# A wider planned margin for what TensorE takes from other engines, and for reused buffers, in the later stages

## The chip, the cores and the metric

The kernel runs on one core of a Trainium2 chip. The metric is the device time of one execution in microseconds. Three runs of the kernel before gave 1037.63, 1038.01 and 1040.27 us; the median is 1038.01 us. One more execution was taken with the hardware profiler; all rows of the profile below come from it. In the rows PE is TensorE's matmuls, PEld its weight loads, DVE is VectorE, ACT is ScalarE, POOL is GpSimd and SP is the engine that issues the DMAs. L1176 is line 1176 of the kernel.

## The reference

Causal attention with a decay bias, and behind it a two-layer network with an ELU between the layers:

```python
batch, n_heads, seq, head_dim = (8, 8, 576, 64)
n_tokens, d_model, d_ff = (4608, 512, 2048)

scores = scale * np.matmul(q, k.transpose(0, 1, 3, 2))
cum = np.cumsum(np.maximum(s, 0.0), axis=-1)
bias = -(cum[:, :, :, None] - cum[:, :, None, :])
scores = np.where(causal, -1000000000.0, scores + np.minimum(bias, 0.0))
scores = scores - np.max(scores, axis=-1, keepdims=True)
attn = np.exp(scores)
attn = attn / (np.sum(attn, axis=-1, keepdims=True) + 1e-09)
x = np.matmul(attn, v)                      # (8, 8, 576, 64)
x = x.transpose(0, 2, 1, 3).reshape(4608, 512)
h = x @ w_in                                # 512 -> 2048
g = np.where(h > 0.0, h, np.exp(np.minimum(h, 0.0)) - 1.0)
out = g @ w_out                             # 2048 -> 512
```

All tensors are 32-bit floats. There are 64 heads (8 batches of 8), and the network sees 4608 tokens of 512 features.

## The kernel before, in words

**Attention.** The work is cut into units. For most batches a unit is one head with up to four blocks of 128 queries. For a block, `softmax_block` (from L1165 on) makes the scores in a PSUM bank by two matmuls (L1176, tiles `kh` and `qs`, then `k` and `q`); VectorE adds the mask, takes the running minimum and empties the bank (L1179, tiles `p` and `mn`); ScalarE takes the exponential (L1189). Then the probabilities are scaled and split into a high and a low half of 16 bits: the high half at L1247, L1249 or L1251 (GpSimd, VectorE or ScalarE), the low half mostly at L1255 on VectorE. SP issues DMA transposes of the halves into `T`, and `heads` (L1396) multiplies them with the values of two heads into the bank `av`. `produce` (L833, L835, L840) turns `av` into the network's input `x`, again in halves. Keys and queries are rounded at L405 and L407, and what is left of them is made at L426 on GpSimd or L425 on VectorE; L1039 makes the low half of the values.

**The network.** Tokens are handled in 18 chunks of 256. A chunk has 8 steps (two blocks of 128 hidden features each). A step has a hidden part, 24 matmuls of 256 columns at L1636 into a bank `h`, issued as 8 operations of three; then ScalarE's exponential (L1654), a subtraction with a limit (L1663 on VectorE or L1659 on ScalarE), VectorE's L1667, the high half `gg` (L1671 or L1673) and its low half (L1676); then the projection, 12 matmuls of 512 columns at L1697 into two banks `o`, as two operations of six. The first chunks (L1573, L1603) use whole 32-bit operands instead. At a chunk's end the banks `o` are copied out (L1734, L1736) and stored.

**PSUM.** Scores, transposes and the small end products share two banks (tag `a`, `N_A` = 2), in the first stages a third one. The hidden parts have two banks and later that third one; the projections have two (`N_O` = 2), `av` has one.

**The order.** All of this is entered as operations in a planner, `Plan`, and `plan.issue()` writes the program. The planner simulates the engines by a cost for each operation (the functions `pe16`, `dve_2` and so on). Again and again it takes, of all operations whose inputs are planned, the one with the earliest start, and among those with the same start the one with the smallest priority number. Its start is the latest of three: when its engine is free (`free`), when its inputs are known there (`ready`, the planned end of each input plus a handover of `HOPS` that depends on the two engines, 150 ns if not listed), and when a slot of each new buffer is free (`slot_free`, the end of the last user plus `HOP` = 150 ns). On TensorE attention comes first by priority (small numbers, in the order of the units), the network's matmuls have 10000 plus the chunk's number, so they fill in what attention leaves. On the other engines the network's own work (-1000 plus the chunk) comes ahead of attention's. Where an operation can be done by several engines, the planner takes the one where it ends first.

What is written is an order for each engine, which the engine keeps; the real waits are semaphores and depend on the data alone. So a number in the planner changes what stands ahead of what, and never adds a wait by itself. A planned time has no meaning on the chip beyond that order.

Two constants already depend on the planned time of TensorE: `THIRD_T` (165 us) moves the third bank from scores to hidden parts, and `FIRST_T` (180 us) changes a weight in the choice of engines.

Of the kernel before, what the change touches and what calls it, by code (L numbers as in the profile page):

```python
# [54 lines left out]
N_FREE = 0  # L55
N_EARLY, N_AUX, N_URGENT = 2, 4, 1

FILL_T, GAP = 60e3, 350.0

N_FILL = 300  # L60
# [29 lines left out]
class Plan:  # L90
# [14 lines left out]
        ("Pool", "Pool"): 50.0,  # L105
    }
    HOP = 150.0

    BIAS = {"DVE": 1.3, "DVE-SB": 1.3}
    FIRST_BIAS = {"DVE": 1.3, "DVE-SB": 1.3}  # L110
# [59 lines left out]
        return o  # L170

    def ready(self, o, engine):
        return max(
            (t + (0.0 if e is None else self.HOPS.get((e, engine), self.HOP))
             for e, t in o.ready.items()),
            default=0.0,
        )

    def issue(self):
        engines = sorted({self.ENGINE.get(w[0], w[0]) for o in self.ops for w in o.ways})  # L180
        port = 0.0
        free = dict.fromkeys(engines, 0.0)
        taken = dict.fromkeys(self.tags, 0)
        slots, skipped = {}, {}
# [2 lines left out]
        def slot_free(key, bufs):  # L187

            held = slots.get(key, ())
            if len(held) < bufs:  # L190
                return 0.0
            was = held[-bufs]
            return None if was.users else was.until + self.HOP

        pending = [o for o in self.ops if not o.left]
        block = self.nc.cur_bb.bb
# [2 lines left out]
        while pending:  # L199
# [12 lines left out]
            for o in pending:  # L212
                t = 0.0
                for b, k in o.new:
                    at = None
                    if b.home_bufs and taken[b.home] == k:
                        b.key, b.bufs = b.home, b.home_bufs
                        at = slot_free(b.key, b.bufs)
                    if b.others and (b.always or not busy):
                        for key, bufs, *rule in b.others:  # L220
                            if rule and not rule[0](taken[key]):
                                continue
                            other = slot_free(key, bufs)
                            if other is not None and (at is None or other < at):
                                at, b.key, b.bufs = other, key, bufs
                    if at is None:
                        break
                    t = max(t, at)
                else:
                    _, n, start = min(  # L230
                        (at + w[1] * bias.get(w[0], 1.0), i, at)
                        for i, w, at in (
                            (i, w, max(t, free[self.ENGINE.get(w[0], w[0])],
                                       self.ready(o, self.ENGINE.get(w[0], w[0])),
                                       port - self.PORT_LEAD[w[0]] if w[0] in self.PORT_LEAD else 0.0))
                            for i, w in enumerate(o.ways)
                        )
                    )
                    rank = (start + GAP if o.filler else start, o.prio)
                    if best is None or rank < best[0]:  # L240
                        best = (rank, o, n)
# [4 lines left out]
            engine, cost, trace = o.ways[n][:3]  # L246
            lag = 0.0
            end = start + cost
            if engine in self.PORT_LEAD:
                port = end  # L250
            engine = self.ENGINE.get(engine, engine)
# [1590 lines left out]
```

## Time and profile before

| | |
|---|---|
| median of 3 runs | 1038.01 us (1037.63 to 1040.27) |
| profiled execution | 1035.61 us, span 1033.7 us |
| busy TensorE / VectorE / ScalarE / GpSimd | 1014.4 / 834.6 / 627.0 / 386.1 us |
| granted clock of TensorE | 1.00 |
| instructions | 21490 |
| largest groups on TensorE | L1697 378.7 us (1608 matmuls), L1636 376.0 us (3072), L1176 with `kh` and `qs` 109.1 us (272) |
| DMA | 137.73 MB, 133 GB/s on average |

A row of a group reads: line, engine, operation, tile written <- tiles read, shape, count, then busy time and mean length in ns, then the engine's idle time just before such instructions and what ended it. In a row of the order of time the first two numbers are start and length in us, and what stands in brackets at the end is the idle time before it with the instruction that ended it. TensorE's matmuls overlap in its pipeline: a matmul of 512 columns has a length of 380 ns, but 36 of them take 7.78 us, 216 ns each.

### The profile page before, as it was taken

The numbers are of one execution on the slowest core, as the hardware profiler recorded it, in microseconds if no ns is written. First come the engines' busy times: TensorE is split into PE (matmuls) and PEld (weight loads), VectorE is DVE, ScalarE is ACT, GpSimd is POOL, SyncE is SP. The second block draws the span as 40 slices with busy tenths as digits, with TensorE's granted clock in tenths as the row PEclk, the third lists the DMA queues.
The fourth block names the chain that finished last, engine by engine and source line by source line (L and its number), as shares of the span: only waits on it lengthen the run. The fifth ranks groups of instructions, "written<-read, shape, count | busy, mean of one in ns | idle before, by whom it ended". The sixth has DMA issues, their size and how long they took to land.

```text
span 1033.7 us, 21490 instructions
## 1 busy us (share of the span) xinstructions
PE 1014.4 (98%) x7260; PEld 695.7 (67%) x7260; DVE 834.6 (81%) x2047; ACT 627.0 (61%) x1502; POOL 386.1 (37%) x605
## 2 busy tenths in 40 slices
PE   8999999999999999999999999999999999999998
PEld 6666766667676666676666666666676766676665
DVE  6889899999989999898899998888888888433333
ACT  4877756676666666766676666756666656333232
POOL 6332345464554445547556444423232322000000
PEclk9999999999999999999999999999999999999999
DMA  7767243779668677766787657747464544100000
GB/s 222 233 198 234 62 142 96 175 155 217 130 146 172 131 151 152 186 149 142 162 201 146 148 132 172 151 109 181 112 141 101 129 110 122 34 22 22 1 21 21
DMA packets 277693, 137.73 MB, mean 133 GB/s; under 512 B 211640, under 2 KB 254928, under 8 KB 277584
## 3 DMA queue, kind: packets, MB, share of 16 engines
q1 hardware_dynamic: 277584, 136.37, 54.8%
q8 instruction: 57, 0.93, 0.4%
q14 instruction: 52, 0.43, 0.1%
HBM read 68.63 MB, written 9.88 MB: 76 GB/s over the span
## 4 chain that ended last, share of the span: by engine, by line
PE 84%; DVE 9%; issue 3%; DMA 2%; ACT 1%; POOL 0%; SPq 0%; DVEq 0%; ACTq 0%; POOLq 0%
PE h L1636 30%; PE o L1697 30%; PE sc L1176 10%; PE av L1396 5%; PE o L1603 3%; PE h L1573 3%; DVE p L1255 2%; DVE v L1039 1%; DMA stk<-in_kT_dram 1%; PE trl L975 1%; PE avl L991 1%; DVE p L1179 1%; PE scratch L1760 1%; DVE g L1663 1%; DMA vs<-in_vb_dram 1%
## 5 line engine op out<-in xcount | busy, mean ns | idle before, releaser
L1697 PE MATMUL o<-wp,gg 128*128 128x512 f16 x1608 | 378.7, 380 | 1.0 <-DVE gg L1676 0.8
L1636 PE MATMUL h<-x,wp 128*128 128x256 f16 x3072 | 376.0, 273 | 0.0
L1636 PEld LDWEIGHTS <-wp 128*128 128x128 f16 x3216 | 301.8, 98 | 65.4 <-issue 8.4
L1697 PEld LDWEIGHTS <-gg 128*128 128x128 f16 x1608 | 151.3, 98 | 158.0 <-issue 3.9
L1255 DVE SCALAR_TENSOR_TENSOR p<-p,sm,p 128x512 f16<-128x512 f32 (+3 forms) x234 | 181.1, 789 | 5.3 <-POOL p L1247 2.4
L1189 ACT ACTIVATE p<-p,mn 128x192 f32<-128x192 f32 (+1 forms) x232 | 143.4, 619 | 43.8 <-DVE mn L1179 41.8
L1654 ACT ACTIVATE g<-h,cs 128x512 f32<-128x512 f32 x134 | 91.7, 684 | 111.5 <-PE h L1636 109.2
L1671 ACT ACTIVATE gg<-h,wc 128x512 f16<-128x512 f32 x122 | 83.6, 685 | 96.7 <-DVE h L1667 96.0
L1179 DVE CUSTOM_DVE_ANT_0 p<-sc,maskw 128x192 f32<-128x192 f32 (+1 forms) x232 | 109.2, 477 | 17.4 <-PE sc L1176 14.1
L1676 DVE SCALAR_TENSOR_TENSOR gg<-h,wc,gg 128x512 f16<-128x512 f32 x134 | 99.8, 745 | 25.8 <-ACT gg L1671 25.1
L1176 PE MATMUL sc<-kh,qs 128*128 128x192 f32 (+2 forms) x272 | 109.1, 405 | 7.0 <-DVE mn L1179 5.6
L1247 POOL TENSOR_SCALAR p<-p,sm 128x512 f16<-128x512 f32 (+3 forms) x105 | 61.1, 586 | 145.4 <-DVE sm L1198 104.0
L1667 DVE SCALAR_TENSOR_TENSOR h<-g,cs,h 128x512 f32<-128x512 f32 x134 | 100.6, 751 | 16.2 <-ACT g L1659 12.1
L1663 DVE TENSOR_SCALAR g<-g 128x512 f32<-128x512 f32 x77 | 37.2, 483 | 74.4 <-ACT g L1654 74.1
L1251 ACT ACTIVATE p<-p,sm 128x512 f16<-128x512 f32 (+3 forms) x114 | 67.6, 603 | 32.4 <-DVE sm L1198 30.9
L1176 PE MATMUL sc<-k,q 128*128 128x192 f32 (+2 forms) x272 | 83.2, 309 | 0.0
L1176 PEld LDWEIGHTS sc<-kh,qs 128*128 128x128 f32 x272 | 51.4, 189 | 28.4 <-DVE mn L1179 7.3
L426 POOL TENSOR_TENSOR qs<-stq,qs 64x512 fp32r<-64x512 f32 (+1 forms) x53 | 63.5, 1198 | 6.7 <-ACT qs L407 1.2
L426 POOL TENSOR_TENSOR k<-stk,kh 64x576 fp32r<-64x576 f32 x36 | 54.8, 1523 | 15.3 <-ACT kh L407 11.8
L1396 PE MATMUL av<-T,v 128*64 128x256 f16 (+5 forms) x896 | 60.3, 286 | 0.0
L405 POOL TENSOR_SCALAR qs<-stq 128x512 fp32r<-128x512 f32 (+1 forms) x42 | 27.9, 664 | 72.9 <-DMA stq<-in_qT_dram 51.6
L1176 PEld LDWEIGHTS sc<-k,q 128*128 128x128 f32 x272 | 51.8, 190 | 1.9
(216 smaller groups left out, 1326.1 us busy)
## 6 DMA issues: line engine op xcount, KB each, us to landing
stk<-in_kT_dram SPq DMA_DIRECT2D x64, 288.0 KB
va<-in_vb_dram SPq DMA_DIRECT2D x32, 320.0 KB
stq<-in_qT_dram SPq DMA_DIRECT2D x40, 256.0 KB
w_raw<-in_w_in_dram SPq DMA_DIRECT2D x16, 512.0 KB
w_raw<-in_w_out_dram SPq DMA_DIRECT2D x16, 512.0 KB
out_dram<-ost SPq DMA_DIRECT2D x32, 256.0 KB
q<-qs SPq DMA_DIRECT2D x40, 128.0 KB
T<-p SPq DMA_TRANSPOSE x208
```

Of the source, the lines that this page charges most:

```text
L426: ("Pool", pool_2(n), lambda: pool.tensor_tensor(dst(), src(), hi(), ALU.subtract)),
L1176: pe_.matmul(view(sc.v[:, :cw]), l, r, start=n == 0, stop=n == len(pairs) - 1)
L1179: op(prio, [("DVE", 84 + dve_p(cw), lambda i=i, sc=sc: dve.tensor_tensor_reduce(pt.v[:, i * cw : (i + 1) * cw], sc.v[:, :cw], mv(i * cw, c ...
L1189: op(prio, [("ACT", 480 + w / 1.2, lambda: act.activation(pt.v[:, :w], pt.v[:, :w], AF.Exp, bias=mn.v[:, at : at + 1], scale=-1.0, accum_o ...
L1255: ("DVE-SB", dve_2(n), lambda part=part: dve.scalar_tensor_tensor(part(t16, 1), own(part), by(part), part(t16, 0), ALU.mult, ALU.subtract)),
L1396: pe_.matmul(av.v[w.h * HB : (w.h + 1) * HB, dst], w.values.v[:, w.h, kb, v], part(w, kb, m), start=n == 0, stop=n == len(order) - 1,)
L1636: pe_.matmul(hp.v[:, m], weight_part(f, 0, part)[1]()[:, c * P : (c + 1) * P], x.v[:, xx, c, o : o + TC], start=(c == 0 and i == 0), stop= ...
L1654: op(side, [("ACT", act_c(2 * TC) + 90, lambda: act.activation(gt.v, flat(hp.v), AF.Exp, scale=by(BACK)))], [hp, (cs[ch], g)], [gt])
L1667: op(side, [("DVE", dve_b(2 * TC), lambda: dve.scalar_tensor_tensor(flat(hp.v), gt.v, by(MINUS if sign[0] else FIRST), flat(hp.v), ALU.mul ...
L1671: ("ACT", act_c(2 * TC) + 90, lambda: act.activation(flat(gg.v[:, 0]), flat(hp.v), AF.Copy, scale=down())),
L1676: op(side, [("DVE", dve_b(2 * TC), lambda: dve.scalar_tensor_tensor(flat(gg.v[:, 1]), flat(hp.v), down(), flat(gg.v[:, 0]), ALU.mult, ALU. ...
L1697: pe_.matmul(acc[i].v, gg.v[:, a, m, i * P : (i + 1) * P], weight_part(2 * fp + m, 1, part)[1](), start=(first and m == 0 and k == 0), sto ...
```

## The change

Two constants come in. `MORE` is 800 ns, and `MORE_T` is 250 us of planned time on TensorE (`self.now`, which `issue` sets to the planned time when TensorE is free). As long as that time is at most `MORE_T`, nothing is different. Behind it, `ready` adds 800 ns to the handover of every input that another engine makes for an operation of TensorE (the DMA queue counts as another engine, TensorE itself does not), and `slot_free` adds 800 ns to the handover of every reused buffer, in PSUM or SBUF, for whichever engine its next user runs on. `issue` sets `self.now` to 0 at its start, since `slot_free` now reads it.

```diff
+MORE_T = 250e3
+
...
     HOP = 150.0
+
+    MORE = 800.0
...
     def ready(self, o, engine):
+        more = self.more() if engine == "PE" else 0.0
         return max(
-            (t + (0.0 if e is None else self.HOPS.get((e, engine), self.HOP))
+            (t + (0.0 if e is None else self.HOPS.get((e, engine), self.HOP) + more * (e != "PE"))
              for e, t in o.ready.items()),
             default=0.0,
         )
 
+    def more(self):
+        return self.MORE if self.now > MORE_T else 0.0
+
     def issue(self):
         engines = sorted({self.ENGINE.get(w[0], w[0]) for o in self.ops for w in o.ways})
-        port = 0.0
+        port = self.now = 0.0
...
             was = held[-bufs]
-            return None if was.users else was.until + self.HOP
+            return None if was.users else was.until + self.HOP + self.more()
```

## The prediction

> **What bounds the kernel now.** I read the page's busy shares first, then the busy time by stages, then TensorE's own waits, then the order of time around the longest of them.
>
> ```profile
> span 1033.7 us, 21490 instructions
> ...
> PE 1014.4 (98%) x7260; PEld 695.7 (67%) x7260; DVE 834.6 (81%) x2047; ACT 627.0 (61%) x1502; POOL 386.1 (37%) x605
> ...
> PE 84%; DVE 9%; issue 3%; DMA 2%; ACT 1%; POOL 0%; SPq 0%; DVEq 0%; ACTq 0%; POOLq 0%
> ```
>
> TensorE is busy in 98% of the span and carries 84% of the chain that ended last. A share of that size leaves little to win; how little is read by stages (columns: stretch, length, then busy time and instruction count of each engine, the granted clock, the DMA share and GB/s).
>
> ```profile
> 250.00:400.00 150.00, 148.99 (x1128) 102.56 (x1125) 136.21 (x343) 97.86 (x242) 73.42 (x107) 1.00 0.70 150
> 400.00:600.00 200.00, 194.11 (x1472) 132.77 (x1471) 178.69 (x459) 131.09 (x332) 110.01 (x158) 1.00 0.72 161
> 600.00:900.00 300.00, 298.73 (x2288) 205.19 (x2287) 248.64 (x587) 185.30 (x418) 90.80 (x134) 1.00 0.54 126
> 900.00:1034.00 134.00, 129.06 (x884) 86.19 (x882) 46.75 (x72) 40.60 (x62) 0.00 (x0) 1.00 0.05 17
> ```
>
> After 250 us TensorE idles 1.0 us, 5.9 us and 1.3 us in the three stretches up to 900 us, 8.2 us together. The clock is at its full 1.00 throughout, so no clock is to be won. VectorE is nearly full as well from 250 to 600 us (136.2 of 150, 178.7 of 200). The last stretch is network alone: its 129.06 us are all that there is up to the last matmul (1029.07, from the chain's last row further down), so TensorE does not idle there at all. The 8.2 us have names (line that waited, line it waited for, total, times, longest):
>
> ```profile
> PE sc L1176 <- DVE mn L1179: 5.6, 9, 1.3
> PE sc L1176 <- DVE x L840: 1.3, 1, 1.3
> PE o L1697 <- DVE gg L1676: 0.8, 1, 0.8
> PE peaks L649 <- DVE tops L641: 0.3, 1, 0.3
> ```
>
> This is the window from 250 to 1034 us: 12 waits, 8.0 us. Ten are scores whose PSUM bank VectorE had not yet emptied, that is, a buffer's reuse; one is a projection whose input VectorE had not yet written, that is, another engine's result. Both are what the change speaks of. The five longest, with what VectorE and GpSimd did ahead of two of them:
>
> ```profile
> 408.61 0.42 PE L1176 MATMUL sc<-kh,qs 128*128 128x320 f32 x1 [1.30 <-DVE mn L1179]
> ...
> 437.44 1.04 PE L1697 MATMUL o<-wp,gg 128*128 128x512 f16 x4 [0.83 <-DVE gg L1676]
> ...
> 486.46 1.47 POOL L426 TENSOR_TENSOR k<-stk,kh 64x576 fp32r<-64x576 f32 x1
> ...
> 486.60 1.89 DVE L1255 SCALAR_TENSOR_TENSOR p<-p,sm,p 128x512 f16<-128x512 f32 x1
> ...
> 489.33 0.40 PE L1176 MATMUL sc<-kh,qs 128*128 128x288 f32 x1 [1.30 <-DVE x L840]
> ...
> 498.80 2.72 DVE L1039 SCALAR_TENSOR_TENSOR v<-va,scales,v 128x320 f16<-128x320 f32 x2
> ...
> 499.63 1.53 POOL L426 TENSOR_TENSOR k<-stk,kh 64x576 fp32r<-64x576 f32 x1
> ...
> 502.11 0.40 PE L1176 MATMUL sc<-kh,qs 128*128 128x288 f32 x1 [1.27 <-DVE mn L1179]
> ...
> 598.26 0.47 PE L1176 MATMUL sc<-kh,qs 128*128 128x448 f32 x1 [1.19 <-DVE mn L1179]
> ```
>
> ```profile
> L1255 DVE SCALAR_TENSOR_TENSOR p<-p,sm,p 128x512 f16<-128x512 f32 (+3 forms) x203 | 155.1, 777 | 4.9 <-POOL p L1247 2.4 <-ACT p L1251 1.5
> ...
> L1176 PE MATMUL sc<-kh,qs 128*128 128x288 f32 (+3 forms) x233 | 93.1, 403 | 6.9 <-DVE mn L1179 5.6 <-DVE x L840 1.3
> ```
>
> VectorE's subtraction at L1255 takes 777 ns on average and took 1.89 us where GpSimd's L426 ran beside it, about 1.1 us more. The code's cost for it (160 + 1.06 ns an element, 703 ns for 512) knows nothing of that meeting. So the written order has TensorE arrive at a score at the planned moment while VectorE is a microsecond late. TensorE takes its work in the written order, so a whole row of ready network matmuls stands behind that one score.
>
> **The change, part by part.** No instruction is added or removed, and no wait on the chip: the planner's numbers alone change, and with them the order (on all queues, SP's included) and here and there the engine that is chosen. Past 250 us of the plan's own clock (the trace does not show that clock; I take it for the trace's, and the five longest waits lie behind 400 us in any case), an operation of another engine counts as known to TensorE 0.8 us later, and a buffer's slot as free 0.8 us later for every engine.
>
> *The stalls.* A score or projection that would be put at the moment when its input is due is now put 0.8 us later, and the network's matmuls that are ready go ahead of it. Each of today's waits should lose up to 0.8 us. The five long ones (1.30, 1.30, 1.27, 1.19, 0.83: 5.9 us) would lose 4.0 us and keep 1.9 us; the other seven share 8.0 - 5.9 = 2.1 us, 0.3 each, and would go wholly. That is 6.1 us of gain. The ends: all 8.0 us, if the scores that suffered move clear of the meetings; 0, if the meetings only strike other scores as hard. The new order will have its own meetings, since L1255, L1039 and L426 are all still there. I let 3.0 us of waits stay, between the 1.9 above and 4.0 (half of today's), and take **-5.0 us**.
>
> One rule speaks against the change here. The Trainium skill (SBUF — State Buffer, Who interferes with whom) has VectorE and GpSimd share a port pair as an exclusive lock, the later one being blocked until the earlier instruction has ended. That fits the 1.89 us beside a 1.47 us L426. By that rule a meeting may cost VectorE a whole L426 (1.53 us), so each of the four long waits could keep 0.7 us rather than 0.4 to 0.5, and the gain would be about 1 us less.
>
> *What the moved scores cost.* A score's first matmul does not always take the same time until the next one starts:
>
> ```profile
> 311.81 1.46 PE L1697 MATMUL o<-wp,gg 128*128 128x512 f16 x6
> 312.92 0.48 PE L1176 MATMUL sc<-kh,qs 128*128 128x288 f32 x1
> 313.24 0.29 PE L1176 MATMUL sc<-k,q 128*128 128x288 f32 x1
> ...
> 414.87 0.30 PE L1176 MATMUL sc<-k,q 128*128 128x288 f32 x1
> 415.01 0.29 PE L1176 MATMUL sc<-kh,qs 128*128 128x288 f32 x1
> 415.14 0.29 PE L1176 MATMUL sc<-k,q 128*128 128x288 f32 x1
> ```
>
> Behind a projection the step is 0.32 us, behind another score 0.13 us, at the same width. So the same 233 scores cost more or less by what stands ahead of them: 0.19 us for each that changes sides. A change of one score in fifteen, 16 of 233, is 3.0 us either way. Nothing says which way: both banks' release moves by the same 0.8 us. I take 0 and keep ±3 us.
>
> The Trainium skill (TensorE: Matmul & The Clock Gate, Architectural detail: the array is 16× 32×32, not 1× 128×128) lets TensorE pull weight loads ahead of matmuls in flight. By that rule alone the neighbour would not matter and this term would be 0 with no bounds. The 0.32 against 0.13 us do not agree with it for these pairs.
>
> *Attention as a whole.* Everything in it that passes through TensorE or takes a used buffer comes up to 0.8 us later in the plan: the scores, behind them VectorE's L1179, ScalarE's exponential, the products L1255, SP's transposes, the weighted values, and the loads that wait for a staging buffer. What hides this is the network, which always has matmuls ready as long as it stands well behind attention:
>
> ```profile
> L833 ACT ACTIVATE x<-av x38: 203/369/573, 270.9 to 900.1; 128x256 f16<-128x256 f32 x23, 128x128 f16<-128x128 f32 x6, 128x192 f16<-128x192 f32 x4, 128x448 f16<-128x448 f32 x3
> ```
>
> ```profile
> 1016.05 5.24 PE h L1636 x48
> 1021.29 7.78 PE o L1697 x36
> ```
>
> The last piece of the network's input is made at 900.1 us. A step's hidden part is 2.62 us (5.24 for 48 matmuls), its projection 2.59 us (7.78 for 36). The last chunk has 8 steps, and its last hidden part ends at 1021.29. With six projections between its hidden parts it began at 1021.29 - 8 x 2.62 - 6 x 2.59 = 984.8 us. So attention may end 84.7 us later before the last chunk waits: 13% of the 650 us since 250 us. I take 0 for this term; if the cover is gone, the price is in the rivals.
>
> *The last stage.* There the chain from a hidden part to its projection is
>
> ```profile
> L1654 ACT ACTIVATE g<-h,cs 128x512 f32<-128x512 f32 x134 | 91.7, 684 | 111.5 <-PE h L1636 109.2
> ...
> L1676 DVE SCALAR_TENSOR_TENSOR gg<-h,wc,gg 128x512 f16<-128x512 f32 x134 | 99.8, 745 | 25.8 <-ACT gg L1671 25.1
> ...
> L1667 DVE SCALAR_TENSOR_TENSOR h<-g,cs,h 128x512 f32<-128x512 f32 x134 | 100.6, 751 | 16.2 <-ACT g L1659 12.1
> ...
> L1663 DVE TENSOR_SCALAR g<-g 128x512 f32<-128x512 f32 x77 | 37.2, 483 | 74.4 <-ACT g L1654 74.1
> ```
>
> and L1671 with about L1654's duration: 684 + 483 + 751 + 684 + 745 = 3.35 us and six handovers. Between a hidden part and its own projection lie another projection and another hidden part, 5.2 us. With the code's handovers (200, 140, 75, 130, 140, 255: 0.94 us) and 0.8 us more the chain has 5.1 us, which just fits. So the order stays what it is: 0 us. If it did not fit, the plan's clock alone would wait, and on the chip the same two kinds of work would alternate.
>
> **The sum.** -5.0 + 0 + 0 + 0 = -5.0 us (+-3 for the neighbours). The profiled execution took 1035.6 us, 1.9 us around its 1033.7 us span; less 5.0 it is 1030.6 us. It lies 2.4 us under the median of the runs shown, 1038.0, so on the median's footing the forecast is **1033.0 us**.
>
> **The rivals.** (1) *The stalls only change places.* For it: the meetings of L1255 and L1039 with L426 are neither fewer nor shorter, and VectorE, 90% busy, gets its scores later too. Against it: the plan now holds 0.8 us of room at every handover into TensorE and every reused bank, and seven of the twelve waits are far below that. Gain about 1 us: 1037 us.
>
> (2) *Attention becomes too slow, and the network runs dry* (the slower side). The scores pass through two banks, each now counted as held 0.8 us longer. If that hold rather than VectorE sets attention's pace, 233 scores x 0.8 us / 2 banks = 93 us of stretch, 8.5 us beyond the cover of 84.7 us, in which TensorE has nothing to do: 1038.0 + 8.5 = 1046.5 us. It decides where the last input piece comes later than 984.8 us. Against it: the scores need a bank for far less than the 2.8 us that lie between two of them (650 us / 233), so the longer hold is mostly slack; and a slower attention takes load from VectorE where that is at 90%.
>
> (3) *The neighbours turn out badly*: more scores behind projections, the 3 us against the gain of 5.0 or against that of rival 1: between 1036 and 1040 us.
>
> (4) *The change does nothing*, since the plan's TensorE is never late and the order stays: 1038 us. Against it: 0.8 us is longer than a projection's three matmuls, so the order must change.
>
> **How the numbers follow.** Less than 0.3%, 3.1 us, cannot be told from no change here. Forecast 0.56; rival 1 0.22, rival 2 0.10, rival 3 0.09, rival 4 0.03. Faster takes the forecast and a little of rival 3's good side: 0.57. Same takes rivals 1 and 4 and some of 3: 0.29. Slower takes rival 2 and the rest of 3: 0.14. The low end is all 8.0 us and the neighbours' 3: 1027 us. The high end goes half-way to rival 2, 1042 us, which leaves out most of that rival and little else. The likeliest case's own range is 1028 to 1035 us.
>
> **What would show it.** TensorE's waits after 250 us fall from 8.0 us to about 3, and none is longer than 1 us; the 400 to 600 stretch rises from 194.1 to 197 us or more busy. The last x at L833 comes between 900 and 950 us. The time of the last stage's matmuls stays at 109 and 216 ns a matmul (2.62 us / 24, 2.59 us / 12). The forecast is wrong if the waits on L1179 keep their 5.6 us, if the neighbours' mean (403 ns at L1176) rises, or if x's last piece passes 985 us and waits for x stand ahead of L1636.

## The result, and the profile after

The changed kernel takes 1024.35 us (median of 4 runs, 1023.63 to 1025.09) against 1037.82 us (4 runs, 1035.5 to 1040.27) for the kernel before: a ratio of 0.987 with a 95% interval of 0.9846 to 0.9894, 13.5 us less. The forecast was 1033.0 us and the range ended at 1027.0, so the direction was right and the size was not. The profiled execution of the changed kernel took 1023.86 us, 11.75 us less than the one of before.

The page of the changed kernel comes first. Behind `issue` its line numbers are 8 higher than before: L1176 is now L1184, L1179 is L1187, L1255 is L1263, L1039 is L1047, L1636 is L1644.

```profile
span 1022.1 us, 21542 instructions
...
PE 1011.3 (99%) x7260; PEld 697.8 (68%) x7260; DVE 819.2 (80%) x2047; ACT 619.4 (61%) x1485; POOL 410.0 (40%) x629
...
PE 92%; DVE 4%; issue 1%; DMA 1%; ACT 1%; POOL 0%; SPq 0%; DVEq 0%; POOLq 0%; ACTq 0%
```

TensorE has the same 7260 matmuls. Its idle time fell from 1033.7 - 1014.4 = 19.3 us to 1022.1 - 1011.3 = 10.8 us, that is by 8.5 us. Its *busy* time fell too, from 1014.4 to 1011.3 us, by 3.1 us for the same work. Together they are the 11.6 us of the span. The second number was in no forecast. The end of a matmul in the profile is modelled and lies well behind the start of the next (a 512-column matmul shows 380 ns, and 216 ns pass from one to the next), so a short stall between two matmuls counts as busy, and a long one is shown shorter than it was. Counting from start to start avoids this. From 250 us on, the steps from a network matmul into a score's first matmul add up to 15.6 us before (153 steps, 12 of them over 0.3 us) and to 4.7 us after (151 steps, one over 0.3 us).

The stages of the changed kernel, in the columns of the prediction's table:

```profile
250.00:400.00 150.00, 150.00 (x1136) 103.32 (x1135) 127.57 (x335) 97.84 (x235) 72.85 (x106) 1.00 0.70 150
400.00:600.00 200.00, 199.90 (x1499) 137.82 (x1498) 174.28 (x457) 127.55 (x317) 95.07 (x137) 1.00 0.66 149
600.00:900.00 300.00, 300.00 (x2326) 208.28 (x2324) 248.28 (x599) 187.50 (x431) 131.63 (x183) 1.00 0.61 137
900.00:1034.00 134.00, 117.90 (x808) 78.76 (x805) 45.19 (x72) 32.45 (x48) 0.00 (x0) 0.99 0.03 13
```

From 250 to 900 us TensorE idles 0.1 us, where it was 8.2 us. The view of TensorE's waits in that window, which had four rows and 8.0 us before, has no row left. The fuller view of the stalls is the idle time ahead of a score's first weight load, since the weight load of a score that waits begins together with its matmul. The score at 489.33 us in the prediction's fourth fence is one: both start there, with 1.30 us shown idle ahead of the matmul and 1.79 us ahead of the load. Groups by line from 250 us to the end, before:

```profile
L1176 PEld LDWEIGHTS sc<-kh,qs 128*128 128x128 f32 x233 | 44.0, 189 | 25.7 <-issue 6.9 <-DVE mn L1179 6.9 <-DVE x L840 1.8
```

and after:

```profile
L1263 DVE SCALAR_TENSOR_TENSOR p<-p,sm,p 128x512 f16<-128x512 f32 (+3 forms) x192 | 141.4, 748 | 4.0 <-POOL p L1255 2.1 <-ACT p L1259 1.6
...
L1184 PE MATMUL sc<-kh,qs 128*128 128x288 f32 (+3 forms) x232 | 93.7, 407 | 0.1
...
L1184 PEld LDWEIGHTS sc<-kh,qs 128*128 128x128 f32 x232 | 43.9, 189 | 14.6 <-issue 3.4 <-DVE mn L1187 0.6 <-DVE k L433 0.3
```

25.7 - 14.6 = 11.1 us: nearly the whole 11.6 us lies in front of the scores. The view puts most of it down to VectorE (L1179 6.9 to 0.6 us, L840 1.8 us to none) and 3.5 us to "issue", that is, to no instruction that it could name.

VectorE is still made late by GpSimd. In the order of time of the changed kernel:

```profile
528.35 1.33 POOL L434 TENSOR_TENSOR qs<-stq,qs 64x512 fp32r<-64x512 f32 x1
...
528.47 1.76 DVE L1263 SCALAR_TENSOR_TENSOR p<-p,sm,p 128x512 f16<-128x512 f32 x1
...
532.50 1.40 POOL L434 TENSOR_TENSOR k<-stk,kh 64x576 fp32r<-64x576 f32 x1
...
532.74 1.70 DVE L1263 SCALAR_TENSOR_TENSOR p<-p,sm,p 128x512 f16<-128x512 f32 x1
...
533.84 0.45 PE L1184 MATMUL sc<-kh,qs 128*128 128x448 f32 x1
```

Two such meetings within 5 us, and the score behind them has no bracket: no wait is shown ahead of it. Before, one meeting (1.89 us at 486.60) was followed by a wait of 1.30 us.

### The profile page after: what moved, and what is told of

The parts are those of the page before. It is cut to its first block, busy times and chain, and to the rows that moved or that the text cites. A ratio compares the mean times of both kernels' runs of the same rounds, so it can differ in the third digit from the quotient of the medians.

```text
span 1022.1 us, 21542 instructions
## 1 busy us (share of the span) xinstructions
PE 1011.3 (99%) x7260; PEld 697.8 (68%) x7260; DVE 819.2 (80%) x2047; ACT 619.4 (61%) x1485; POOL 410.0 (40%) x629
## 4 chain that ended last, share of the span: by engine, by line
PE 92%; DVE 4%; issue 1%; DMA 1%; ACT 1%; POOL 0%; SPq 0%; DVEq 0%; POOLq 0%; ACTq 0%
PE h L1644 33%; PE o L1705 33%; PE sc L1184 10%; PE av L1404 5%; PE o L1611 3%; PE h L1581 3%; PE trl L983 1%; PE avl L999 1%; PE scratch L1768 1%; DVE p L1263 1%; DMA vs<-in_vb_dram 0%; DMA w_raw<-in_w_out_dram 0%; PE avn L1422 0%; PE sc_n L1330 0%; DMA stk<-in_kT_dram 0%
## 5 line engine op out<-in xcount | busy, mean ns | idle before, releaser
L1644 PE MATMUL h<-x,wp 128*128 128x256 f16 x3072 | 374.8, 273 | 0.0
L1644 PEld LDWEIGHTS <-wp 128*128 128x128 f16 x3216 | 303.0, 98 | 66.3 <-issue 7.4
L1263 DVE SCALAR_TENSOR_TENSOR p<-p,sm,p 128x512 f16<-128x512 f32 (+3 forms) x223 | 167.7, 766 | 4.3 <-POOL p L1255 2.1
L1255 POOL TENSOR_SCALAR p<-p,sm 128x512 f16<-128x512 f32 (+3 forms) x127 | 78.8, 626 | 203.3 <-DVE sm L1206 154.2
L1187 DVE CUSTOM_DVE_ANT_0 p<-sc,maskw 128x192 f32<-128x192 f32 (+1 forms) x232 | 109.5, 479 | 28.4 <-PE sc L1184 27.1
L1184 PE MATMUL sc<-kh,qs 128*128 128x192 f32 (+2 forms) x272 | 109.9, 407 | 0.3 <-DVE mn L1187 0.2
L1671 DVE TENSOR_SCALAR g<-g 128x512 f32<-128x512 f32 x90 | 41.5, 461 | 73.9 <-ACT g L1662 73.2
L1259 ACT ACTIVATE p<-p,sm 128x512 f16<-128x512 f32 (+3 forms) x104 | 65.1, 630 | 35.7 <-DVE sm L1206 34.1
L1184 PE MATMUL sc<-k,q 128*128 128x192 f32 (+2 forms) x272 | 83.0, 309 | 0.0
L434 POOL TENSOR_TENSOR qs<-stq,qs 64x512 fp32r<-64x512 f32 (+1 forms) x53 | 63.0, 1189 | 17.9 <-ACT qs L415 11.4
L434 POOL TENSOR_TENSOR k<-stk,kh 64x576 fp32r<-64x576 f32 x39 | 59.0, 1512 | 15.8 <-ACT kh L415 6.9
L1184 PEld LDWEIGHTS sc<-kh,qs 128*128 128x128 f32 x272 | 51.5, 189 | 17.9 <-issue 3.8
L1184 PEld LDWEIGHTS sc<-k,q 128*128 128x128 f32 x272 | 51.8, 190 | 2.1
L1404 PEld LDWEIGHTS <-v 128*64 128x64 f16 x896 | 39.5, 110 | 19.9 <-issue 9.3
```

Of the source, the lines that this page charges most:

```text
L434: ("Pool", pool_2(n), lambda: pool.tensor_tensor(dst(), src(), hi(), ALU.subtract)),
L1184: pe_.matmul(view(sc.v[:, :cw]), l, r, start=n == 0, stop=n == len(pairs) - 1)
L1187: op(prio, [("DVE", 84 + dve_p(cw), lambda i=i, sc=sc: dve.tensor_tensor_reduce(pt.v[:, i * cw : (i + 1) * cw], sc.v[:, :cw], mv(i * cw, c ...
L1263: ("DVE-SB", dve_2(n), lambda part=part: dve.scalar_tensor_tensor(part(t16, 1), own(part), by(part), part(t16, 0), ALU.mult, ALU.subtract)),
L1404: pe_.matmul(av.v[w.h * HB : (w.h + 1) * HB, dst], w.values.v[:, w.h, kb, v], part(w, kb, m), start=n == 0, stop=n == len(order) - 1,)
L1644: pe_.matmul(hp.v[:, m], weight_part(f, 0, part)[1]()[:, c * P : (c + 1) * P], x.v[:, xx, c, o : o + TC], start=(c == 0 and i == 0), stop= ...
```

## The experiments

Four questions were open: which of the two places of the margin does it, whether the engines chosen anew do it, whether the size of the margin does it or any new order would, and whether VectorE's lateness is the cause at all. All times are medians of 4 runs or more; the kernel before, timed again beside each group of them, stood at 1036.7 to 1038.0 us, and the ratios are against those runs. "Waits" are TensorE's waits from 250 us on, as in the prediction's third fence. "Meetings" are VectorE's instructions of L1255 and L1039 longer than 1.2 us in that window, counted in the trace (36 before, 26 in the changed kernel; alone a 128x512 one takes 0.74 us). At every one of them GpSimd was at work at the same time.

### The two places of the margin

`e1_ready_only` keeps the margin in `ready` alone, `e2_slots_only` in `slot_free` alone, `e17_banks_only` in `slot_free` for PSUM's pool alone.

```diff
# e1_ready_only
-            return None if was.users else was.until + self.HOP + self.more()
+            return None if was.users else was.until + self.HOP
# e2_slots_only
-        more = self.more() if engine == "PE" else 0.0
+        more = 0.0
# e17_banks_only: as e2_slots_only, and
-            return None if was.users else was.until + self.HOP + self.more()
+            return None if was.users else was.until + self.HOP + self.more() * (key[0] == self.signal[0])
```

> Only TensorE's inputs from other engines are counted 0.8 us later; a reused buffer's slot keeps its 150 ns. Theory 1 (room at a bank's reuse is what counts, since 10 of the 12 waits of before were scores waiting for a bank): most of the waits on L1179 stay, 5 us or more of TensorE idle time after 250 us, and a time of 1033 to 1038 us. Theory 2 (room at TensorE's inputs is enough, since the late VectorE delays inputs and banks alike): under 2 us idle and 1024 to 1028 us.

> Only reused buffers are counted free 0.8 us later; TensorE's inputs keep their handovers. Theory 1: nearly all of the gain, 1024 to 1028 us, the waits of scores on L1179's bank gone and at most one or two projections waiting for L1676. Theory 2: under half of the gain, 1031 us or more.

> The 0.8 us is added for reused PSUM banks alone: not for buffers in SBUF, and not for TensorE's inputs. If room at the banks' reuse is the whole of it (10 of the 12 waits of before were for a bank): 1024 to 1028 us, waits on L1187 under 1.5 us. If the room in SBUF's buffers, which holds attention's loads and other engines back, has a share: 1029 to 1033 us, the level of the draws without room.

Measured: 1028.57 us (ratio 0.9914, 0.9898 to 0.9931) with inputs alone, 1025.32 us (0.9877, 0.9862 to 0.9892) with all slots, 1030.26 us (0.9934, 0.9918 to 0.9951) with banks alone. TensorE's waits with inputs alone:

```profile
PE sc L1184 <- DVE mn L1187: 1.7, 5, 0.7
PE sc L1184 <- DVE sm L1206: 1.1, 1, 1.1
```

With all slots the view has no row. With banks alone:

```profile
PE sc L1184 <- DVE mn L1187: 1.3, 3, 0.7
PE o L1705 <- DVE gg L1684: 1.0, 2, 0.8
PE av L1404 <- DMA T<-p: 0.7, 1, 0.7
PE peaks L657 <- DVE tops L649: 0.3, 1, 0.3
```

Inputs alone fell between the two theories, with 2.8 us of waits left. The slots are worth more than the inputs, as theory 1 had it, but not for its reason: the banks alone give hardly more than a new order does by itself (below). By these runs the slots of SBUF's buffers have the larger share (1030.26 - 1025.32 = 4.9 us), although TensorE waited for a bank in 10 of 12 waits. But each is a single order, and orders without room lie 2.1 us apart, so the shares are rough. Which of those buffers it is was not tried.

### The engines chosen anew

The margin also changes which engine does an operation: GpSimd's instructions went from 605 to 629, ScalarE's from 1502 to 1485, and VectorE's busy time from 834.6 to 819.2 us. `e3_margin_old_engines` holds the choices of the kernel before and has the margin; `e4_new_engines_no_margin` holds those of the changed kernel and has none.

```diff
+CHOICES = ( ... )     # one digit for each operation with a choice
...
+        several = [o.prio[1] for o in self.ops if len(o.ways) > 1]
...
+        chosen = {k: int(n) for k, n in zip(several, CHOICES)}
...
-                            for i, w in enumerate(o.ways)
+                            for i, w in enumerate(o.ways) if i == chosen.get(o.prio[1], i)
```

> The full margin, but each operation that several engines can do stays on the engine that it had in the kernel before; the order alone may change. Theory A (order: the gain is room in TensorE's order): 1024 to 1029 us, TensorE's waits after 250 us under 2 us. Theory B (balance: the gain is the work that went from VectorE to GpSimd, VectorE's 834.6 to 819.2 us busy): 1033 us or more.

> No margin, but each operation that several engines can do is put on the engine that it has in the changed kernel. Theory A: no gain, 1034 to 1040 us, 6 us or more of waits on TensorE after 250 us. Theory B: most of the gain, 1023 to 1029 us.

Measured: 1023.85 us (0.9871, 0.9856 to 0.9886) and 1025.57 us (0.9882, 0.9867 to 0.9897). The first says that the new balance is not needed. The second went against theory A: without the margin there should have been no gain. Neither theory alone holds both. The wait view of `e4_new_engines_no_margin` has one row, and the stretch from 400 to 600 us shows what is different:

```profile
PE sc L1199 <- DVE mn L1202: 0.4, 1, 0.4
```

```profile
400.00:600.00 200.00, 200.00 (x1515) 138.58 (x1514) 164.73 (x445) 125.06 (x312) 94.30 (x135) 1.00 0.62 144
```

VectorE is busy 164.7 us there, where it was 178.7 us, and both kernels with held choices have 14 meetings instead of 36. Perhaps a planner that must wait for a given engine leaves gaps on VectorE; that was not shown. In any case this run is no neutral control: it has less lateness, where the margin leaves room for it. The idle time ahead of a score's weight load is 15.8 us in it (25.7 before), so here too it is the stalls that went. That the missing meetings are its whole gain was not shown separately.

### The size of the margin, and new orders without room

`MORE` alone is changed. With 20 ns the order behind 250 us is a new one (the last piece of `x` comes at 878.8 us instead of 900.1), but there is no room in it.

```diff
-    MORE = 800.0
+    MORE = 20.0        # 10, 50, 100, 400, 700, 1000, 1600, 2400
```

> MORE 20 ns instead of 800: the plan behind 250 us is reshuffled as thoroughly as by 800 ns, but there is no room worth the name. Theory M (the margin does it, by its size): 1033 to 1040 us, 6 us or more of TensorE waits after 250 us. Theory D (the plan of before was an unlucky draw, and any other draw is better): 1023 to 1030 us, waits under 3 us.

> MORE 100 ns, a second nearly neutral draw. Theory M: 1032 to 1039 us (a hundred nanoseconds off each of 12 waits is 1.2 us). Theory D: 1023 to 1030 us.

> MORE 50 ns, a third nearly neutral draw beside 20 and 100 ns (1031.2 and 1032.2 us). If the order of before was an unlucky draw by some 5 us: 1029 to 1034 us. If 20 and 100 ns were the lucky ones: 1035 us or more.

> MORE 10 ns, a fourth nearly neutral draw. If draws without room lie at 1031 to 1032 us as 20, 50 and 100 ns did: 1029 to 1034 us. If they spread so far that the kernel before is an ordinary one: 1035 us or more.

> MORE 400 ns, half the margin. Theory M: about half of the gain, 1028 to 1033 us, waits of 2 to 5 us left. Theory D: 1023 to 1030 us, no trend against 20 and 100 ns.

> MORE 700 ns, a second draw with nearly the full room. If the room sets the time: 1023 to 1027 us, waits after 250 us under 2 us. If the changed kernel's 1024 us was a lucky draw: 1028 us or more.

> MORE 1000 ns, a third draw with the full room. If the room sets the time: 1022 to 1026 us, waits under 1 us. If the changed kernel's 1024 us was a lucky draw: 1028 us or more.

> MORE 1600 ns. Theory M: no waits are left to remove beyond 800 ns, so 1022 to 1026 us, unless attention is slowed until the network runs dry: then waits of L1644 for x and 1030 us or more, with the last piece of x behind 985 us. Theory D: 1022 to 1030 us, where in this range does not follow from the margin.

> MORE 2400 ns, three times the margin. The prediction's rival 2 (attention slowed until the network runs dry) decides where the last piece of x comes later than about 42 us before the last hidden part ends. With 1600 ns it came at 945.7 us (before: 900.1), 46 us later for 1600 ns. If that goes on in proportion, 2400 ns brings it to 970 us: still covered, 1022 to 1026 us. If the two score banks, then held 2.4 us longer each, set attention's pace: 1050 us or more, with TensorE idle for lack of x between 400 and 1000 us.

The column "load" is the idle time ahead of a score's first weight load from 250 us on.

| MORE, ns | us | ratio, 95% | waits, us | load, us | meetings |
|---|---|---|---|---|---|
| 0 (before) | 1037.82 | 1 | 8.0 | 25.7 | 36 |
| 10 | 1033.31 | 0.9962, 0.9943 to 0.998 | 6.1 | 23.7 | 35 |
| 20 | 1031.24 | 0.9944, 0.9929 to 0.9959 | 5.1 | 21.2 | 21 |
| 50 | 1031.75 | 0.9946, 0.9926 to 0.9965 | 4.1 | 20.5 | 31 |
| 100 | 1032.22 | 0.995, 0.9932 to 0.9968 | 4.6 | 20.7 | 26 |
| 400 | 1027.41 | 0.9912, 0.9892 to 0.9932 | 1.6 | 19.1 | 32 |
| 700 | 1026.66 | 0.9904, 0.9882 to 0.9926 | 0.5 | 15.2 | 34 |
| 800 (the change) | 1024.35 | 0.987, 0.9846 to 0.9894 | 0 | 14.6 | 26 |
| 1000 | 1024.65 | 0.9887, 0.9863 to 0.9911 | 0 | 16.0 | 21 |
| 1600 | 1023.61 | 0.9877, 0.9856 to 0.9897 | 0 | 17.1 | 20 |
| 2400 | 1045.64 | 1.0082, 1.0064 to 1.01 | 14.6 | 23.1 | 9 |

Both theories hold a part, and with 20 ns neither range held. Four orders without room stand at 1031.2 to 1033.3 us, 1032.1 on average: the order of before was a worse draw than any of them, by 5.7 us on that average. The four with 700 to 1600 ns stand at 1023.6 to 1026.7 us, 1024.8 on average: the room is worth 1032.1 - 1024.8 = 7.3 us. By the ratios instead of the medians the two parts are 5.1 and 6.8 us.

The column "load" says what most of both parts consists of, from one profiled execution of each: 25.7 us before, 21.5 us on average without room, 15.7 us with it. So a new order by itself has fewer stalls ahead of scores, by 4.2 us, and the room takes another 5.8 us of the same kind. The luck of the draw is then in the main no second mechanism beside the stalls; it decides how many of them an order has.

The pair that tells best that it is the room has nearly the same meetings, 35 and 34. (The profiled execution with 10 ns took 1036.85 us, the longest of ten with a median of 1033.31, so its waits may be more than usual for it.) TensorE's waits with 10 ns:

```profile
PE sc L1184 <- DVE mn L1187: 3.7, 6, 1.3
PE sc L1184 <- DVE mn_n L1334: 1.1, 1, 1.1
PE av L1404 <- DMA T<-p: 0.7, 1, 0.7
PE avn L1422 <- DMA T<-p: 0.3, 1, 0.3
PE o L1705 <- DVE gg L1684: 0.3, 1, 0.3
```

and with 700 ns:

```profile
PE avn L1422 <- DMA T<-p: 0.3, 1, 0.3
PE sc L1184 <- DVE mn L1187: 0.2, 1, 0.2
```

With 700 ns VectorE is as full from 400 to 600 us, where most of the waits stood, as it was before (179.0 against 178.7 us), so it is not a relief of VectorE there either.

```profile
400.00:600.00 200.00, 199.81 (x1506) 137.15 (x1502) 179.05 (x465) 135.41 (x334) 100.89 (x141) 1.00 0.71 159
```

At 2400 ns the prediction's rival 2 came true, and much earlier than at the last chunk. The last piece of `x` is made at 987.4 us, but TensorE already runs out of work behind 510 us. From 400 to 600 us it idles 11.2 us, from 600 to 900 us 3.7 us. Two of those stretches:

```profile
510.00:520.00 10.00, 7.12 (x34) 4.08 (x33) 8.49 (x26) 5.49 (x15) 2.25 (x4) 0.81 0.65 162
520.00:530.00 10.00, 6.39 (x49) 4.85 (x47) 7.92 (x23) 4.19 (x13) 3.63 (x6) 0.68 0.87 166
```

In the order of time of TensorE there, with the last scores and the weighted values that finish a batch:

```profile
517.01 0.61 PE L1184 MATMUL sc<-kh,qs 128*128 128x288 f32 x1 [1.06 <-DVE x L848]
...
523.57 3.46 PE L1404 MATMUL av<-T,v 128*64 128x512 f16 x27 [3.46 <-DMA T<-p]
...
528.40 1.48 PE L1644 MATMUL h<-x,wp 128*128 128x256 f16 x12
```

No hidden part runs from 510 us until 528.40; that batch's last high halves of `x` were made at L841 from 527.1 us on. The expectation had carried the 46 us of delay at 1600 ns on in proportion, and failed.

### VectorE made late on purpose

In both kernels the second of the two instructions of L1039 for a pair of heads is issued twice, with the same result. The planner counts it once, so order and engines stay.

```diff
-                ("DVE-SB", dve_2(n // 2), lambda h=h: dve.scalar_tensor_tensor(
-                    low()[:, h], src()[:, h], by(), high()[:, h], ALU.mult, ALU.subtract)),
+                ("DVE-SB", dve_2(n // 2), lambda h=h: [dve.scalar_tensor_tensor(
+                    low()[:, h], src()[:, h], by(), high()[:, h], ALU.mult, ALU.subtract) for _ in range(1 + h)]),
```

> The kernel before, with VectorE made late on purpose: for every second half of the values the instruction L1039 is issued twice (same result), which the planner does not count; order and engines stay. That is some 27 instructions of about 0.7 us. If the mechanism is a late VectorE in front of a score without room, a good part of each goes straight to TensorE: 5 to 15 us slower than before, 1042 to 1052 us, with TensorE waiting 13 us or more after 250 us. If VectorE's lateness is not what sets the time: within 3 us of before.

> The changed kernel with the same doubled instruction. If the margin's room absorbs up to 0.8 us of lateness at each handover: 0 to 3 us slower than the changed kernel, 1024 to 1027 us, TensorE waits under 3 us. If the changed kernel is only a luckier order without more room: as much slower as the kernel before, 5 to 15 us, 1029 to 1039 us.

Measured: 1049.3 us (1.012, 1.0098 to 1.0143), 11.4 us more than before, and 1027.66 us (0.9908, 0.9889 to 0.9927), 3.3 us more than the changed kernel. In the kernel before the instruction's count went from 54 to 83 and TensorE's waits from 8.0 to 15.1 us; the two longest groups:

```profile
PE sc L1176 <- DVE mn L1179: 12.8, 15, 1.8
PE avn L1414 <- DVE mn L1179: 1.1, 1, 1.1
```

In the changed kernel the count went from 56 to 86, and one row of waits is left:

```profile
PE sc L1184 <- DVE mn L1187: 1.1, 2, 0.7
```

Part of its 3.3 us may lie ahead of 250 us, where it has no margin. There TensorE's busy time fell from 143.84 + 99.63 to 142.94 + 98.88 us, by 1.65 us; but kernels that share the order up to 250 us of planned time show 240.3 us (50 ns) to 244.4 us (20 ns) in their profiles, so this is not told from noise. Lateness of VectorE does go to TensorE, then, and the changed order does take most of it up. Of all runs these bear most on the mechanism, since the order is the same in each pair. The same doubling in an order without room other than that of before was not run.

### The margin earlier

```diff
-MORE_T = 250e3
+MORE_T = 0e3         # e12_from_0; 150e3 in e16_from_150
```

> The margin of 800 ns from the start, MORE_T 0. In the first 250 us TensorE idles 6.3 us in the changed kernel's profile (240 - 233.9 would be too many to cover: most of it lies in the first 100 us, where attention alone runs and the network has nothing ready). If the margin costs nothing where cover is thin: 1022 to 1026 us. If it delays attention where nothing hides it: 1028 us or more, with the idle time before 150 us grown.

> The margin of 800 ns from 150 us on, where the network's 16-bit matmuls begin. If the loss of the margin from the start (6 us against the changed kernel) came from the first 150 us, where the network has little to put in: 1021 to 1026 us. If it came from behind 150 us: 1027 us or more.

Measured: 1030.57 us (0.993, 0.9907 to 0.9953) and 1025.57 us (0.9891, 0.9866 to 0.9916). From the start the margin costs 6.2 us against the changed kernel, from 150 us on 1.2 us, which its interval does not tell from none. The loss has a row, in the first 100 us. The changed kernel:

```profile
L1768 PE MATMUL scratch<-ident 128*128 128x128 f32 x86 | 14.5, 317 | 0.0
```

and with the margin from the start:

```profile
L1768 PE MATMUL scratch<-ident 128*128 128x128 f32 x138 | 20.4, 292 | 0.0
```

These transposes are idle work that the planner puts in where it sees TensorE free. It saw it free 52 times more, and 20.4 - 14.5 = 5.9 us of busy time went into nothing. They fill a pause that attention leaves: its first pieces of `x` at L848 come at 67.3 us instead of 56.5 us. That the delay and not the transposes themselves costs the time was not shown separately. None of the 18 kernels is faster than the change beyond its interval.

## Why the prediction was right or wrong

**What bounds the kernel: right.** TensorE's waits for VectorE were what could be won, and the waits for banks and inputs went, all of them.

**The stalls: the mechanism was right and the term of -5.0 us was mis-sized; it measured 11.6 us on the profiled span, 11.1 us of it ahead of scores.** Three things were wrong in it. First, "I let 3.0 us of waits stay": none stayed. Second, "the ends: all 8.0 us" took the wait rows for everything that could be won. They count from a matmul's modelled end; 3.1 us more stood in TensorE's busy time, and the idle time ahead of the score's weight load (25.7 us, of which 11.1 us went) would have shown it. Third, the term took the stalls of the order of before for what any order has. The size series splits the gain of 13.5 us in 5.7 us for a new order without room (the average of four) and 7.3 us for the room, with 0.5 us between the average of the series and this order. The forecast had nothing for the first part, and that its 5.0 us come near the second is chance, since it had worked them out from the waits of before.

"No instruction is added or removed" holds for TensorE's 7260 matmuls; in all there are 52 instructions more (21542 for 21490), with other choices of engine on GpSimd and ScalarE.

The step from the profiled execution to the median added 1.7 us: the profiled execution of before lay 2.2 us under the median of its 4 runs, that of after 0.5 us.

**"Knows nothing of that meeting": wrong as put.** `PORT_LEAD` in the planner does keep VectorE's work on SBUF and GpSimd's apart in planned time, except for a lead of 0.24 and 0.12 us, before as after. On the chip 36 meetings happened all the same, so the queues did not keep to the planned times. What the plan lacks is not the rule but anything that holds the engines to it.

**The rule on the shared port: the lengths agree, the price did not.** It said that a meeting can cost a whole L426, more than the margin holds, and so 1 us less gain. The two meetings shown of the changed kernel agree with it in length (1.70 and 1.76 us against 0.74 alone, beside GpSimd instructions of 1.40 and 1.33 us), but TensorE shows no wait behind any of the 26, and the gain was larger than forecast, not smaller. That a margin sits at several handovers in a row would explain it, and 400 ns already brought the waits to 1.6 us; which handovers take it up was not shown.

**The neighbours of a score: right.** Directly behind another score stood 43 of the 233 scores before and 42 of 232 after, and the steps from a score's first matmul to its second add up to 56.3 us before and 57.0 us after: 0.7 us, well within the +-3 us. The sign that the prediction named, the mean length of 403 ns, did rise, to 407 ns (0.9 us over 233), without the forecast failing there.

**Attention as a whole: 0 was right, the cover was counted at the wrong place.** In the changed kernel the last piece of `x` came at 899.3 us instead of 900.1, a little ahead of the 900 to 950 us that the prediction named:

```profile
L841 ACT ACTIVATE x<-av x37: 218/384/597, 268.7 to 899.3; 128x256 f16<-128x256 f32 x24, 128x64 f16<-128x64 f32 x4, 128x128 f16<-128x128 f32 x4, 128x448 f16<-128x448 f32 x3
```

and the network had caught up by the stalls' 11 us. But the 84.7 us of cover belong to the last chunk. At 2400 ns the network ran dry in the middle, at 510 us, where less stands between a batch's attention and its first chunk. The decision point "later than 984.8 us" was not the one that decided.

**The last stage: right**, 2.62 and 2.59 us a step as before:

```profile
1004.89 5.24 PE h L1644 x48
1010.13 7.78 PE o L1705 x36
```

**The rivals.** Rival 1 (other stalls in their place, 1 us of gain) was wrong in its size: orders without room kept 4 to 6 us of waits and still gained 4.5 to 6.6 us. Rivals 3 and 4 did not happen. Rival 2 did not happen up to twice the margin, and did at three times.

## What to carry to other kernels

Where a written order feeds one full engine from another that can be late, plan each handover and each reuse of a buffer later than the model says, as long as the full engine has other ready work; here 0.7 to 1.6 us at a step of 5.2 us were worth 7 us, and where there was no other work (the first 100 us) the same margin cost 6 us. Before believing such a gain, time a few reshuffles without the effect: a margin of 10 to 100 ns already gained 5 us, because the order of before was a poor draw: it had more of the same stalls than the four others. And read the room for improvement from the idle time ahead of the weight loads, since waits counted from a matmul's modelled end leave a part of the stalls in the busy time.

## What the runs showed of the hardware that was not expected

A TensorE that pauses is slowed beyond the pause. In the run with 2400 ns the granted clock was 1.00 up to 516 us, 0.54 from 516 to 518, 0.50 from 518 to 526, and 1.00 again from 528 us on. From 524 to 526 us TensorE was busy all the time and still had 0.50. A score's matmul at 517.01 shows 0.61 us where the same shape shows 0.38 us elsewhere. The clock fell before the longest pause: ahead of the fall, from 512 to 516 us, TensorE was busy 2.1 of 4 us, with 1.54 us as the longest single pause, and the pause of 3.46 us ended at 523.57, when the clock was already low.

The Trainium skill (TensorE: Matmul & The Clock Gate, What's actually happening) has the clock halved after an idle window of about 3.4 us. The trace agrees with the half. It does not show a whole idle window ahead of the fall: here a stretch that was idle about half of the time was enough, and how idle it has to be was not measured. In the kernels before and after, whose pauses behind 250 us are at most 1.3 us, the clock stayed at 1.00 until the last matmuls were done.

VectorE loses time beside GpSimd often, and TensorE need not notice: 20 to 36 VectorE instructions of 1.2 to 2.0 us stood in every order up to 1600 ns (9 with 2400 ns), where a 128x512 one takes 0.74 us alone, and in four of these orders TensorE's waits came to less than one microsecond.
